# A fused attention and gated-MLP layer on one core: one hand-written order of all work, buffer places and load queues exchanged for another

## The chip, the cores and the metric

The kernel runs on one NeuronCore of a Trainium2 chip. A core has five engines that run side by side: PE (TensorE, matrix products), DVE (VectorE), ACT (ScalarE), POOL (GpSimd) and SP (SyncE, which here only issues DMA transfers). Each engine works through its own list of instructions strictly in order, and waits at an instruction until the semaphores that it names are up. The metric is the device time of one execution in microseconds (us). The kernel before takes 272.52 us, the median of three runs (272.19 to 273.63).

## The reference

Everything is bfloat16; S = 2048 rows, D = 640, H = 32 heads of 20, F = 1536.

```python
x = A_x
h  = x + A(layernorm(x))          # linear attention with a two-sided softmax feature map
h2 = h + B(layernorm(h))          # bilinear gated MLP, no nonlinearity
# A: q, k, v = split(x @ wqkv) by heads
#    pq = q @ w_phi[head];  pk = k @ w_phi[head]
#    phi_q = [softmax(pq), softmax(-pq)];  phi_k = [softmax(pk), softmax(-pk)]
#    kv = sum over rows phi_k^T v;  z = sum over rows phi_k
#    o = (phi_q @ kv) / (phi_q . z + 1e-6);  return o @ wo
# B: return ((x @ w_gate) * (x @ w_up)) @ w_down
```

## The kernel before

The 2048 rows are cut into 16 tiles t of 128 rows. Names of operations are a letter code and the tile's number; where a fold or a weight block is meant, the block's number.

- **Opening.** x0, x1, ... load rows; wk0 to wk4, wv0 to wv4, w5 (the feature matrices), wo, wg, wu, wd load weights. warm0 to warm19 are matmuls on zeros that nothing reads. WT0 to WT4 transpose the key weights on PE, WTe copies them out, Ph0 to Ph2 (POOL) spread the feature matrices, and F1_0 to F1_4 multiply the two ("fold"), so that one product gives pk directly; Fe1 copies the fold into the weight tile Wp. F0_0 to F0_4 do the same for the queries; their operand, the transposed query weights (tile scratch), comes by five DMA transposes wqt0 to wqt4, and each F0 waits for all five.
- **Norm and transposition.** L1s, L1a (DVE) take mean and variance of a tile, L1l and L1e (ACT) make the reciprocal deviation, L1n (POOL or DVE) the offset that an xn on ACT needs, xn scales the tile (DVE, or ACT with a longer instruction), xt transposes it into xnT: tiles 0 and 1 on PE with a copy xte, all others by a DMA transpose of SP.
- **Keys and values.** K, V on PE (ten matmuls of 320 columns each); Kx two exponentials on ACT, Ks the sums on DVE, Kr and Ke their reciprocal on ACT, Kn the product on POOL; Ve copies V out; KV adds the tile's contribution to the sum over rows. KVe0, KVe1 (DVE) close that sum, and all N need it.
- **Queries.** Q on PE, Qx (ACT), Qs (DVE), Qr (ACT), Qb (POOL), Qe (ACT), Qn (POOL), qT (DMA transpose), then N on PE; dd, rd, o on DVE, oT (DMA transpose), O on PE, h (DVE) adds to x; hc (ACT or DVE) and hT (DMA transpose) bring h into xnT for the MLP.
- **MLP.** For five blocks of rows (256, 512, 512, 512, 256) and twelve blocks of 128 inner columns: U_0 (gate) and U_1 (up) on PE, g copies the gate (ACT), u multiplies (DVE); then D on PE per tile, y (DVE), w stores.

No planner runs at build time. A table of text (PLAN) gives each operation a place in one global list, for some the engine (a second number), and the places of its PSUM banks or SBUF buffers (numbers behind the last colon). `arrange` sorts by that place; each engine's list is the sorted list cut down to that engine, and a wait is put in for each true dependence and each reuse of a buffer or bank. SP's list is at the same time the order in which SP issues transfers; loads whose second number is 1 are issued by ACT, or by SP where ACT is the first choice.

```python
        k, a, o.slots = PLAN.get(name, (key, 0, ()))
        o.eng, o.occ, o.lat = o.alts[a]
        ...
    for o in sorted(G.ops, key=lambda o: (o.key, o.i)):
```

Of the kernel before, what the change touches and what calls it, by code (L numbers as in the profile page):

```python
# [53 lines left out]
zero:0 x0:1:1 id0:2 w5:3:1 eps:4 warm0:5 gl0:6 x3:7:1 wk0:8 warm1:9 warm2:10 gla:11 wk1:12 warm3:13 id1:14 warm4:15 warm5:16 glb:17 x1:18 warm6:19 ekz:20  # L54
warm7:21 va1:22 wk2:23:1 warm8:24::0 warm9:25 wk3:26 warm10:27 warm11:28 wv0:29:1 warm12:30 L1s0:31 warm13:32 Ph0:33 wk4:34:1 warm14:35 warm15:36 warm16:37
x2:38 Ph1:39 L1a0:40 warm17:41 L1s3:42 WT1:43::7 L1l0:44 wv1:45 warm18:46 L1e0:47 Ph2:48 warm19:49 WTe1:50:1 wv4:51:1 xn0:52::3 Sz:53 mk0:54 wv3:55 L1a3:56
L1s1:57 phz:58 xt0:59::1 x4:60 F1_1:61::2 xte0:62 WT0:63::5 L1a1:64 wv2:65:1 WT2:66::0 L1l1:67 WTe0:68:1 x6:69 L1l3:70 WT3:71::7 L1e1:72 WTe2:73:1 Fe1_1:74
F1_0:75::4 xn1:76::3 F1_2:77::0 L1e3:78 Fe1_0:79:1 WTe3:80 L1n3:81 WT4:82::2 xt1:83::3 xn3:84::0 Fe1_2:85:1 F1_3:86::6 xte1:87:1 K0_0:88::4 xt3:89 Fe1_3:90
K0_1:91 WTe4:92:1 K0_2:93 L1s2:94 V0_0:95::0 F1_4:96::2 wqt0:97 V1_0:98::6 Fe1_4:99:1 V1_1:100 L1s4:101 K0_3:102 V1_2:103 K1_0:104::2 L1a2:105 L1s5:106
wqt3:107 L1l2:108 K1_1:109 K0_4:110 L1e2:111 K1_2:112 L1n2:113:1 L1a4:114 K1_3:115 L1a5:116 xn2:117::2 L1l4:118 K1_4:119 V0_1:120 L1e4:121 Kx0_0:122::0  # L60
xt2:123 V0_2:124 L1n5:125:1 L1n4:126 xn5:127::3 V0_3:128 Kx0_1:129 V0_4:130 L1s6:131 V1_3:132 Kx1_0:133::1 V1_4:134 x10:135 V3:136::4 L1s7:137 Kx1_1:138
xt5:139 Ve1:140::0 L1a6:141 xn4:142::0 K3:143::2 Ks0:144::0 Ve3:145::1 x8:146 Ve0:147::2 xt4:148 K2:149::4 L1a7:150 Ks1:151::1 L1l6:152 Kx3_0:153::2 wqt4:154
Kx3_1:155 V2:156::0 L1s11:157 L1e6:158 Kx2_0:159::3 L1n6:160 wqt1:161 L1n7:162 Kr0:163 Ks3:164::2 Kx2_1:165 K5:166::2 Ke0:167 Kr1:168 wqt2:169 Ve2:170::3
Kn0:171 xn6:172::3 V5:173::4 xn7:174:1:2 L1s9:175 xt6:176 Kx5_0:177::4 Ks2:178::3 V4:179::6 Ke1:180 Kx5_1:181 Kn1:182 xt7:183 Ve5:184::4 L1s8:185 F0_4:186::2
Kr2:187 Kr3:188 F0_3:189::0 Ke2:190 x14:191 Fe0_4:192:1 K4:193::4 Fe0_3:194 x12:195 L1a9:196 L1a8:197 Kn2:198 Ve4:199::5 Ks5:200::1 wo2:201 KV0:202::2,3
L1l8:203 L1e8:204 F0_2:205::0 Kx4_0:206::0 V6:207::6 L1n9:208:1 L1n8:209:1 xn9:210::0 Kx4_1:211 L1s10:212 rqz:213 xt9:214 Fe0_2:215 KV1:216 Ke3:217 L1a11:218
F0_0:219::4 Kr5:220 xn8:221::1 Kn3:222 K7:223::0 Fe0_0:224 Ks4:225::3 xt8:226 Ve6:227::0 F0_1:228::4 Kx7_0:229::1 L1a10:230 wg0:231 KV2:232 L1s14:233
K6:234::6 Kr4:235 wu1:236 mk1:237 Kx7_1:238 L1s15:239 Ke4:240 Fe0_1:241 Kn4:242 L1a14:243 KV3:244 Ks7:245::2 L1l10:246 K9:247::0 Kx6_0:248::3 Kx6_1:249
L1s13:250 L1e10:251 Ke5:252 Q0_0:253::4 Kx9_0:254::2 Q0_1:255 Kn5:256 L1n10:257:1 Q1_0:258::6 L1a13:259 L1s12:260 Kx9_1:261 Q1_1:262 Q0_2:263 Q1_2:264
xn10:265:1:0 L1a15:266 Q0_3:267 L1a12:268 Ks6:269::3 Q1_3:270 Q1_4:271 L1l12:272 xt10:273 Kr7:274 Q0_4:275 L1e12:276 Ke7:277 K8:278::0 L1n11:279 Qx1_0:280::3  # L70
Kn7:281 Ks9:282::1 Qx1_1:283 wo0:284 KV4:285 Kr6:286 wg2:287 Qx0_0:288::1 KV5:289 Qs1:290 Q3:291::6 Qx0_1:292 L1n13:293 L1n15:294 Ke6:295 Kx8_0:296::4
L1n12:297 Kn6:298 Qs0:299 V7:300::4 Kx8_1:301 Qr1:302::2 Qx3_0:303::0 xn13:304::1 Q5:305::0 Qx3_1:306 Ve7:307:1:5 xt13:308 Qb1:309 Qr0:310::0 Kr9:311
L1n14:312 xn15:313::2 Qb0:314 Ke9:315 mk2:316 KV6:317 Kn9:318 Qx5_0:319::2 Ks8:320::3 K10:321::6 wg1:322 xn11:323:1:3 Qs3:324 Qx5_1:325 Q2:326::4 xt11:327
Kr8:328 Qe1:329 smz:330 Kx10_0:331::3 Qn1:332 xn12:333::0 xt15:334 Q9:335::0 Ke8:336 Kx10_1:337 xn14:338::1 Qx2_0:339::4 Qs5:340 Kn8:341 xt12:342 KV7:343
Qx2_1:344 V8:345::6 Qr3:346::1 Qx9_0:347::5 Qs2:348 wg3:349 Qe0:350 K13:351::4 wu2:352 Qb3:353 Ve8:354::5 Qn0:355 Ks10:356::0 Qe3:357 Qx9_1:358 K11:359::6
Kx13_0:360::1 Qn3:361 Kx13_1:362 V9:363::0 Kx11_0:364::0 qT3:365::0 Qr2:366::3 Qr5:367::0 Kr10:368 Qb2:369 Qb5:370 KV8:371 Ke10:372 Kx11_1:373 Ve9:374:1:1
Kn10:375 K12:376::4 xt14:377 Ks13:378::3 V10:379::0 qT1:380::4 Kx12_0:381::4 Ks11:382::1 Kx12_1:383 K15:384::6 Qe5:385 Kr13:386 wd2:387 Ve10:388::6 Qn5:389
Ks12:390::0 qT0:391::1 Ke13:392 Kr11:393 Ke11:394 KV9:395 Qe2:396 Kn13:397 Q4:398::0 Kx15_0:399::2 Qs9:400 qT5:401::2 Kx15_1:402 K14:403::4 Qx4_0:404::0
Ks15:405::2 Kn11:406 Qx4_1:407 KV10:408 Qr9:409::1 V14:410::6 Kx14_0:411::3 Kr15:412 Ke15:413 wu0:414 Q10:415::0 Qb9:416 Ve14:417:1:7 Qn2:418 Qe9:419
Kx14_1:420 Qs4:421 V13:422::6 Kn15:423 Qx10_0:424::1 qT2:425::3 Kr12:426 Ks14:427::1 Ke12:428 Qr4:429::0 V12:430::4 Qx10_1:431 wu3:432 Ve13:433::3 Kn12:434  # L80
Kr14:435 V11:436::0 Ve12:437:1:6 Qs10:438 Q13:439::6 Ve11:440::0 Ke14:441 Kn14:442 V15:443::0 Qx13_0:444::3 Qx13_1:445 KV11:446 Ve15:447::5 Qs13:448 KV12:449
KV13:450 Qn9:451 Qr10:452::2 KV14:453 KV15:454 Q6:455::4 KVe0:456 Qb4:457 qT9:458::5 Qe4:459 Qn4:460 KVe1:461 Qx6_0:462::4 N0:463::2 N2:464::6 dd0:465::1
qT4:466::1 Qx6_1:467 Q7:468::0 rd0:469 dd2:470::0 o0:471::0 Qr13:472::3 rl2:473 Qb13:474 rd2:475 Qb10:476 o2:477::1 N1:478::4 Qx7_0:479::2 Q11:480::2
oT0:481::0 dd1:482::0 Qx7_1:483 rd1:484 o1:485::2 N9:486::6 oT2:487::1 Qx11_0:488::5 N3:489::0 dd9:490::0 Q8:491::4 rd9:492 Qx11_1:493 dd3:494::3 rd3:495
oT1:496::2 Qe13:497 o3:498::0 Qn13:499 O0:500::2 Qx8_0:501::0 oT3:502::3 o9:503::1 Qx8_1:504 O2:505::0 Qe10:506 h0:507 oT9:508::0 Qs7:509 hc0:510::3 N5:511::2
O1:512::4 qT13:513::2 h2:514 Qr7:515::3 Qb7:516 Qn10:517 O3:518::6 h1:519 hT0:520 hc1:521::2 N4:522::0 h3:523 Q14:524::4 L2q1:525 hT1:526 dd5:527::2
dd4:528::0 rl5:529 rd4:530 hc2:531::1 o4:532::1 O9:533::6 rd5:534 qT10:535::0 Qx14_0:536::3 o5:537::0 Qx14_1:538 Q12:539::0 h9:540 oT4:541::0 Qs14:542
U0_1_0:543::2 wd3:544 U0_0_0:545::6 g0_1:546::1 N13:547::4 oT5:548::3 U0_2_0:549::7 Qx12_0:550::1 dd13:551::1 Qs8:552 U0_0_1:553::2 g0_0:554::3 g0_2:555::0
hT2:556 U0_2_1:557::3 Qx12_1:558 U0_5_0:559::7 u0_0:560::0 Qr14:561::2 L2q2:562 rd13:563 Qb14:564 U0_1_1:565::6 wd1:566 hc3:567:1:0 O4:568::0 Qr8:569::0
u0_1:570 o13:571::2 u0_2:572 U0_3_0:573::6 Qs6:574 U0_4_0:575::2 g0_3:576::0 L2q0:577 O5:578::4 h4:579 Qe7:580 g0_5:581::1 Qn7:582 g0_4:583::2 U0_11_0:584::3  # L90
Qe14:585 hc4:586:1:3 h5:587 N10:588::0 U0_3_1:589::7 L2v1:590 qT7:591::2 Qn14:592 L2q5:593 U0_6_0:594::6 u0_3:595 U0_9_1:596::5 dd10:597::2 rd10:598 Qb8:599
hT3:600 U0_5_1:601::4 o10:602::1 L2v0:603 U0_4_1:604::7 U0_7_0:605::2 oT13:606::3 u0_4:607 Q15:608::0 L2v5:609:1 u0_5:610 g0_7:611::0 hc9:612:1:2 g0_6:613::3
hc5:614::1 hT4:615 U0_7_1:616::6 Qr6:617::3 Qx15_0:618::2 U0_6_1:619::7 hT5:620 Qx15_1:621 U0_8_0:622::2 u0_6:623 g0_11:624::2 U0_10_1:625::4 u0_7:626
L2q4:627 Qs12:628 U0_8_1:629::3 g0_8:630::3 U0_9_0:631::7 Qe8:632 Qn8:633 U0_10_0:634::0 u0_8:635 g0_9:636::1 L2q3:637 N7:638::1 U1_3_0:639::6 qT14:640::2
dd7:641::1 u0_9:642 Qb6:643 g0_10:644::3 rd7:645 Qe6:646 Qn6:647 o7:648::0 U1_1_1:649::7 qT8:650::0 L2r5:651 u0_10:652 U1_1_0:653::5 U1_0_1:654::3 oT7:655::0
U1_0_0:656::1 oT10:657::2 U1_2_1:658::0 g1_0:659::1 g1_3:660::0 hT9:661 u1_0:662::1 U1_2_0:663::1 Qs15:664 N8:665::2 g1_2:666::1 U1_7_0:667::6 g1_1:668::3
Qs11:669 U0_11_1:670::4 U1_9_0:671::5 dd8:672::0 u0_11:673 u1_1:674 U1_4_0:675::1 rd8:676 o8:677::0 U1_5_0:678::7 g1_4:679::3 u1_2:680 oT8:681::1 L2q9:682
# [809 lines left out]
```

## Time and profile before

| what | value |
|---|---|
| median of three runs | 272.52 us |
| time of the profiled execution | 272.19 us |
| its span (first to last instruction of the program) | 270.5 us |
| PE busy | 264.4 us, 98% |
| DVE, ACT, POOL busy | 157.0, 123.4, 70.7 us |
| DMA moved | 28.09 MB, mean 104 GB/s |

The span begins at the first instruction of any engine; the remaining 1.7 us of the profiled execution lie outside of it. A page row of waits reads "who waited, on what, total us, times, longest". A row of the timeline reads "start, length, engine, line, operation, number of instructions merged", and in brackets the idle time ahead of it with what the trace takes for its end. Matmul ends are modelled: a following matmul starts up to 0.16 us before the modelled end of the one before.

### The profile page before, as it was taken

How to read it: one execution, taken by the hardware profiler on the slowest of the kernel's cores; microseconds unless marked ns; L12 is line 12 of the kernel's file. 1: busy time of each engine (PE TensorE's matmuls, PEld its weight loads, DVE VectorE, ACT ScalarE, POOL GpSimd, SP SyncE). 2: the span in 40 equal slices, each digit the busy share in tenths (PEclk: the TensorE clock that was granted, in tenths of full speed). 3: DMA queues.
4: the chain of work that ended last, by engine and by line, in shares of the span. 5: the costliest groups of instructions: out<-in, count | busy, mean ns of one | idle time of the engine just before them, and what ended most of it. 6: DMA issues, size and time to landing. Idle time of an engine off the chain costs nothing.

```text
span 270.5 us, 5196 instructions
## 1 busy us (share of the span) xinstructions
PE 264.4 (98%) x2103; PEld 177.5 (66%) x2103; DVE 157.0 (58%) x296; ACT 123.4 (46%) x317; POOL 70.7 (26%) x86
## 2 busy tenths in 40 slices
...
GB/s 202 265 155 182 203 194 168 198 206 204 175 141 112 165 191 127 100 106 133 67 27 153 81 2 72 27 24 73 27 46 102 25 0 2 0 0 1 51 73 73
DMA packets 71752, 28.09 MB, mean 104 GB/s; under 512 B 59056, under 2 KB 71728, under 8 KB 71728
## 3 DMA queue, kind: packets, MB, share of 16 engines
...
q8 instruction: 16, 0.26, 0.4%
q10 hardware_dynamic: 288, 0.33, 0.4%
...
## 4 chain that ended last, share of the span: by engine, by line
PE 83%; DMA 6%; DVE 4%; ACT 3%; SPq 2%; POOL 1%; issue 1%; DVEq 0%
PE ps L646 39%; PE ps L665 19%; PE ps L460 14%; PE ps L603 8%; SPq L263 2%; DMA scratch<-ph 2%; DMA xnT<-xn 2%; DMA x_all<-in_A_x_dram 2%; PE ps L566 2%; ACT ek L472 1%; DVE SR L476 1%; POOL ek L496 1%; PE ps L504 1%; ACT ev L229 1%; DVE st L407 1%
## 5 line engine op out<-in xcount | busy, mean ns | idle before, releaser
L646 PE MATMUL ps<-xnT,Wgu 128*128 128x512 bf16 (+1 forms) x600 | 108.1, 336 | 0.2 <-issue 0.2
L646 PEld LDWEIGHTS ps<-xnT,Wgu 128*128 128x128 bf16 x600 | 58.0, 98 | 42.7 <-DVE ev L654 0.8
L651 ACT ACTIVATE gt<-ps 128x512 bf16<-128x512 f32 (+1 forms) x60 | 29.3, 511 | 97.1 <-PE ps L646 86.1
L460 PE MATMUL ps<-Wp,xnT 128*128 128x320 bf16 (+1 forms) x480 | 68.6, 299 | 0.2 <-DMA xnT<-xn 0.2
L654 DVE TENSOR_TENSOR ev<-ps,gt 128x512 bf16<-128x512 f32 (+1 forms) x60 | 34.0, 579 | 57.7 <-PE ps L646 43.5
L460 PEld LDWEIGHTS ps<-Wp,xnT 128*128 128x128 bf16 x480 | 45.5, 97 | 17.6 <-DMA xnT<-xn 0.3
L665 PE MATMUL ps<-Wd,ev 128*128 128x320 bf16 (+2 forms) x396 | 53.8, 295 | 0.0
L665 PEld LDWEIGHTS ps<-Wd,ev 128*128 128x128 bf16 x396 | 38.2, 98 | 15.4
L496 POOL TENSOR_TENSOR ek<-ek,SR 128x1280 bf16<-128x1280 bf16 x16 | 37.5, 2360 | 3.8 <-ACT SR L481 3.7
L548 POOL TENSOR_TENSOR ph<-ph,RQ 128x660 bf16<-128x660 bf16 x16 | 20.9, 1311 | 28.6 <-ACT RQ L544 28.5
L677 DVE SCALAR_TENSOR_TENSOR Wp<-ps,rs,x_all 128x640 bf16<-128x640 f32 (+3 forms) x18 | 14.3, 806 | 22.7 <-PE ps L665 20.2
L534 DVE TENSOR_REDUCE S<-ph 128x66 f32<-128x1320 bf16 x16 | 24.1, 1520 | 2.1 <-ACT ph L531 2.0
L603 PE MATMUL ps<-Wo,Wp 128*128 128x320 bf16 x160 | 23.5, 299 | 0.0
L529 ACT ACTIVATE ph<-ps 128x600 bf16<-128x600 f32 x32 | 21.4, 683 | 4.0 <-PE ps L460 2.6
L476 DVE TENSOR_REDUCE SR<-ek 128x64 f32<-128x1280 bf16 x16 | 23.2, 1464 | 0.0
L472 ACT ACTIVATE ek<-ps 128x640 bf16<-128x640 f32 x32 | 21.4, 708 | 1.7 <-PE ps L460 1.3
L609 DVE SCALAR_TENSOR_TENSOR x_all<-ps,x_all 128x640 bf16<-128x640 f32 x16 | 13.1, 821 | 12.4 <-PE ps L603 12.4
L603 PEld LDWEIGHTS ps<-Wo,Wp 128*128 128x128 bf16 x160 | 15.6, 98 | 6.6 <-issue 0.2
L624 POOL TENSOR_SCALAR ln<-mv 128x1 f32<-128x1 f32 x6 | 1.2, 192 | 62.3 <-ACT ek L620 62.0
L593 DVE TENSOR_TENSOR o<-ps,sm 128x660 bf16<-128x660 f32 x16 | 13.4, 843 | 4.3 <-ACT sm L586 3.3
L620 ACT ACTIVATE ek<-x_all,mv 128x640 bf16<-128x640 bf16 x16 | 13.2, 823 | 1.2 <-DVE x_all L609 1.2
L618 ACT ACTIVATE xn<-x_all,mv 128x640 bf16<-128x640 bf16 x10 | 8.1, 822 | 6.1 <-DVE x_all L609 6.1
...
## 6 DMA issues: line engine op xcount, KB each, us to landing
...
```

The costliest lines, as they stand in the source:

```text
L460: ins = e.matmul(pb(b, hb)[:, 0:n1 - n0], lhsT=T["xnT"][:, NC - 1 - c, P * t:P * (t + 1)], rhs=T["Wp"][:, POS[kind], c, n0:n1], start=(c = ...
L472: G.op("act", "%sx%d_%d" % (nm, t, s), lambda e, s=s, b=b, ek=ek: e.activation(out=T["ek"][:, ek.slots[0], 0:2 * D].rearrange("p (b h s f) ...
L476: G.op("dve", "%ss%d" % (nm, t), lambda e, ek=ek, sr=sr: e.tensor_reduce(out=T["SR"][:, sr.slots[0], 0, :], in_=T["ek"][:, ek.slots[0], 0: ...
L496: G.op("pool", "Kn%d" % t, lambda e, eng, ek=ek, sr=sr: e.tensor_tensor(out=T["ek"][:, ek.slots[0], 0:2 * D].rearrange("p (h f) -> p h f", ...
L529: e.activation(out=v[:, 0:10].rearrange("p (b g) j f -> p b g j f", b=2), in_=pp(b, 0, 300).rearrange("p b (g j f) -> p b g j f", j=3, f=D ...
L534: G.op("dve", "Qs%d" % t, lambda e, t=t, ph=ph: e.tensor_reduce(out=T["S"][:, t, 0:66].rearrange("p (g k) -> p g k", k=6), in_=pv(ph).rear ...
L548: return e.tensor_tensor(out=v, in0=v, in1=T["RQ"][:, rq.slots[0], 1, 0:33].rearrange("p (g j) -> p g j", j=3).unsqueeze(3).to_broadcast([ ...
L603: ins = e.matmul(pb(b, hb)[:, 0:320], lhsT=T["oT"][:, oT.slots[0], c, :], rhs=T["Wo"][:, c, 320 * hb:320 * (hb + 1)], start=(c == 0), stop ...
L646: ins = e.matmul(pb(b)[:, 0:n], lhsT=T["Wgu"][:, gu, c, P * ft:P * (ft + 1)], rhs=T["xnT"][:, NC - 1 - c, o0:o0 + n], start=(c == 0), stop ...
L651: G.op("act", "g%d_%d" % (bi, ft), lambda e, pg=pg, gt=gt, n=n: e.activation(out=T["gt"][:, gt.slots[0], 0:n], in_=pb(pg)[:, 0:n], func=AF ...
L654: o_ = G.op("dve", "u%d_%d" % (bi, ft), lambda e, pu=pu, gt=gt, hh=hh, ft=ft, n=n: e.tensor_tensor(out=T["hh"][:, hh.slots[0], ft, 0:n], i ...
L665: ins = e.matmul(pb(b, hb)[:, 0:w], lhsT=T["hh"][:, hh.slots[0], ft, P * tt:P * (tt + 1)], rhs=T["Wd"][:, ft, c0 + w * hb:c0 + w * (hb + 1 ...
```

## The change

Only the table is exchanged. The operations, their shapes, their number on each engine's arithmetic and the pools are the same; what differs is the place of every operation, the engine of those with a choice, the buffers, and which queue issues the first loads. The new table has one line of text more, so every line below it has a number higher by one. Of the old and the new table, the beginning, and the places of the fourteenth key tile:

```diff
@@ PLAN, first words
-zero:0 x0:1:1 id0:2 w5:3:1 eps:4 warm0:5 gl0:6 x3:7:1 wk0:8 warm1:9 warm2:10 gla:11 wk1:12
+zero:0 mk0:1 wk1:2:1 x0:3 gl0:4 warm0:5 w5:6 wk0:7:1 id0:8 warm1:9 warm2:10 id1:11 x3:12 x1:13
...
@@ the fourteenth key tile, PE's words alone
-K14:403:4 ... KV10:408 V14:410:6 Q10:415:0 V13:422:6 V12:430:4 V11:435:0 Q13:439:6 V15:443:0 KV11:446
+K14:405::0 ... KV10:411 Q10:414:4 V15:417:2 V12:426:0 V11:432:4 Q13:436:2 V14:441:4 KV11:444
```

SP's list from the first load on. x_all is the tile of the rows, ev holds the key weights here, Wp<-in_A_wqkv the value weights, xnT<-xn an xt, scratch<-in_A_wqkv a wqt. Before:

```order
L263 DMA w5<-in_A_w_phi_dram 128x5x20
L263 DMA x_all<-in_A_x_dram 128x640
L263 DMA ev<-in_A_wqkv_dram 128x640
L263 DMA x_all<-in_A_x_dram 128x640
L263 DMA ev<-in_A_wqkv_dram 128x640 x2
```

Now:

```order
L264 DMA x_all<-in_A_x_dram 128x640
L264 DMA ev<-in_A_wqkv_dram 128x640
L264 DMA x_all<-in_A_x_dram 128x640
L264 DMA ev<-in_A_wqkv_dram 128x640 x3
L264 DMA Wp<-in_A_wqkv_dram 128x640
```

w5 and x3 have left SP's list and x0 and wk0 have entered it: ACT issues wk1, w5, x3 now, and issued x0 and wk0 before.

SP's list further on, from xt3 to xt7. Before:

```order
L449 DMA_TRANSPOSE xnT<-xn 128x5x128
L287 DMA_TRANSPOSE scratch<-in_A_wqkv_dram 128x1x640 x2
L449 DMA_TRANSPOSE xnT<-xn 128x5x128
L263 DMA x_all<-in_A_x_dram 128x2x640
L449 DMA_TRANSPOSE xnT<-xn 128x5x128
L263 DMA x_all<-in_A_x_dram 128x2x640
L449 DMA_TRANSPOSE xnT<-xn 128x5x128
L287 DMA_TRANSPOSE scratch<-in_A_wqkv_dram 128x1x640 x3
L449 DMA_TRANSPOSE xnT<-xn 128x5x128 x2
```

Now:

```order
L450 DMA_TRANSPOSE xnT<-xn 128x5x128
L288 DMA_TRANSPOSE scratch<-in_A_wqkv_dram 128x1x640 x2
L450 DMA_TRANSPOSE xnT<-xn 128x5x128
L264 DMA x_all<-in_A_x_dram 128x2x640 x2
L450 DMA_TRANSPOSE xnT<-xn 128x5x128
L288 DMA_TRANSPOSE scratch<-in_A_wqkv_dram 128x1x640 x3
L450 DMA_TRANSPOSE xnT<-xn 128x5x128 x3
```

The order before is xt3, two wqt, xt2, x10, xt5, x8, xt4, three wqt, xt6, xt7; now both x loads stand ahead of xt5, and the last three wqt ahead of xt4.

ACT's list at its start (L229 and L230 are copies out of PSUM, L429 and L430 an xn). Before:

```order
L414 ACTIVATE ln<-mv,eps 128x1
L417 ACTIVATE rs<-ln 128x1
L229 ACTIVATE scratch<-ps 128x5x128
L229 ACTIVATE xnT<-ps 128x5x128
L414 ACTIVATE ln<-mv,eps 128x1 x2
L417 ACTIVATE rs<-ln 128x1
L229 ACTIVATE Wp<-ps 128x640
L417 ACTIVATE rs<-ln 128x1
L229 ACTIVATE Wp<-ps 128x640 x4
```

Now:

```order
L415 ACTIVATE ln<-mv,eps 128x1
L418 ACTIVATE rs<-ln 128x1
L230 ACTIVATE scratch<-ps 128x5x128
L415 ACTIVATE ln<-mv,eps 128x1
L230 ACTIVATE scratch<-ps 128x5x128
L230 ACTIVATE Wp<-ps 128x640
L415 ACTIVATE ln<-mv,eps 128x1
L418 ACTIVATE rs<-ln 128x1 x2
L230 ACTIVATE Wp<-ps 128x640
L430 ACTIVATE xn<-x_all,nb,rs 128x5x128
L230 ACTIVATE Wp<-ps 128x640
```

xn3 has come from DVE to ACT, behind WTe1, WTe0, Fe1_1 and Fe1_0; WTe0 and WTe4 have come to ACT as well, while xte0 and Fe1_2 have gone to DVE. On PE, the first query folds F0_0 and F0_4 stand behind six products of ten matmuls (V3, K3, V2, K2, V5, K5), where seven (V4 too) stood ahead of the first of them before.

More of the change, by code (lines that the diff above doesn't have):

```diff
@@ L53 @@
 for _t in """
[L54 to L97, printed above, removed]
@@ L122 @@
-D13_0:1004::6 y14_0:1005::0 w14_0:1006 w8_0:1007 D12_0:1008::2 y13_0:1009::2 w13_0:1010 w7_0:1011 D11_0:1012::6 y12_0:1013::0 y15_0:1014::2 w12_0:1015
-D10_0:1016::2 y11_0:1017::1 w11_0:1018 w15_0:1019 D15_1:1020::1 y10_0:1021::0 w10_0:1022 D15_2:1023::6 y15_1:1024::1 w15_1:1025 y15_2:1026::2 w15_2:1027
+zero:0 mk0:1 wk1:2:1 x0:3 gl0:4 warm0:5 w5:6 wk0:7:1 id0:8 warm1:9 warm2:10 id1:11 x3:12 x1:13 warm3:14 warm4:15 gla:16 warm5:17 wk2:18:1 glb:19 warm6:20
+eps:21 phz:22 warm7:23 wk3:24 warm8:25::5 warm9:26 wk4:27:1 warm10:28 warm11:29 wv0:30:1 warm12:31 warm13:32 L1s0:33 x2:34 warm14:35 warm15:36 Ph0:37
@@ new lines @@
+WT1:38::1 wv1:39 warm16:40 L1a0:41 warm17:42 L1s3:43 Ph1:44 x4:45 L1l0:46 L1e0:47 WTe1:48:1 wv2:49:1 Ph2:50 xn0:51::0 wv4:52:1 L1a3:53 rqz:54 va1:55 WT0:56::2
+L1l3:57 x6:58 xt0:59::1 L1s1:60 WTe0:61 F1_1:62::6 WT2:63::0 wv3:64 Fe1_1:65 xte0:66:1 F1_0:67::2 L1a1:68 WT3:69::4 WTe2:70:1 L1l1:71 warm18:72 L1e3:73
+WT4:74::6 WTe3:75 L1e1:76 Fe1_0:77:1 L1n3:78 warm19:79 F1_2:80::0 ekz:81 xn1:82::1 F1_3:83::4 smz:84 xn3:85:1:0 Sz:86 Fe1_2:87 K0_0:88::2 K0_1:89 xt1:90::7
+Fe1_3:91 L1s2:92 xt3:93 K0_2:94 V0_0:95::0 WTe4:96 V0_1:97 xte1:98:1 K0_3:99 L1a2:100 L1s5:101 V0_2:102 wqt2:103 L1l2:104 F1_4:105::4 L1e2:106 K1_0:107::6
```

89 lines of the change are left out of this document (65 added, 24 removed).

## The prediction

> **What bounds the kernel now.** I read the page first, for the share of each engine, and then the waits of PE alone.
>
> ```profile
> span 270.5 us, 5196 instructions
> ...
> PE 264.4 (98%) x2103; PEld 177.5 (66%) x2103; DVE 157.0 (58%) x296; ACT 123.4 (46%) x317; POOL 70.7 (26%) x86
> ```
>
> ```profile
> PE ps L345 <- DVE ev L343: 1.1, 1, 1.1
> PE ps L370 <- DMA ev<-in_A_wqkv_dram: 0.8, 1, 0.8
> PE ps L389 <- ACT SR L481: 0.5, 1, 0.5
> PE ps L440 <- DVE xn L431: 0.4, 1, 0.4
> PE ps L566 <- DMA scratch<-ph: 0.3, 1, 0.3
> PE ps L646 <- issue: 0.2, 1, 0.2
> PE ps L460 <- DMA xnT<-xn: 0.2, 1, 0.2
> ```
>
> PE bounds the kernel: it is busy for 264.4 of 270.5 us. Its waits come to 3.5 us in seven places, 2.3 us of which (L345, L370, L440) lie before its first product of real size. The change takes no matmul away, so the most it can win is these 3.5 us (1.3%) and stalls inside of what counts as busy; what it can lose is open. The question is whether the new order keeps PE fed. The timeline of PE shows two of these places:
>
> ```profile
> 6.53 0.45 PE L440 MATMUL ps<-ident,xn 128*128 128x128 bf16 x5 [0.44 <-DVE xn L431]
> ...
> 25.83 0.80 PE L389 MATMUL ps<-Phi,scratch 128*128 128x140 bf16 x12 [0.55 <-ACT SR L481]
> 26.47 1.52 PE L460 MATMUL ps<-Wp,xnT 128*128 128x320 bf16 x10
> 27.83 0.50 PE L504 MATMUL ps<-ev,ek 128*128 128x63 bf16 x11
> ```
>
> The row at 6.53 is xt0, at 25.83 F0_4 and F0_3, at 26.47 K4, at 27.83 KV0; of the waits above, L460 is K9 and L566 is N9. From start to start, a product of ten matmuls takes 1.36 us (26.47 to 27.83) and a fold 0.32 us (25.83 to 26.47, two of them). The row at 25.83 names ACT, but F0_4 also waits for all five wqt, and the rows below say that the last of them landed 0.2 us before it: the wait is for a DMA.
>
> **The opening and SP's chain.** Both hang on SP's list. Its rows for x3, wk1, x1, xt3, xt4 and the last three wqt:
>
> ```profile
> 1.32 0.51 SPq L263 DMA_DIRECT2D x_all<-in_A_x_dram  x1
> 1.88 0.42 SPq L263 DMA_DIRECT2D ev<-in_A_wqkv_dram  x1
> 2.35 0.43 SPq L263 DMA_DIRECT2D x_all<-in_A_x_dram  x1
> ...
> 9.97 1.31 SPq L449 DMA_TRANSPOSE xnT<-xn  x1
> ...
> 18.62 1.20 SPq L449 DMA_TRANSPOSE xnT<-xn  x1
> 19.86 3.90 SPq L287 DMA_TRANSPOSE scratch<-in_A_wqkv_dram  x3
> ```
>
> From issue to landing the views by tile give, for the three wqt, for xt4, for the next two xt (xt6, xt7), for x3 and for x1, in this order:
>
> ```profile
> DMA to landing us min/median/max: 3.1/3.8/4.5
> DMA to landing us min/median/max: 3.9/3.9/3.9
> DMA to landing us min/median/max: 2.6/2.7/2.7
> DMA to landing us min/median/max: 3.7/3.7/3.7
> DMA to landing us min/median/max: 3.4/3.4/3.4
> ```
>
> The last wqt is issued at 22.49 (a third of the 3.90 before that row's end) and lands 3.1 later, at 25.6; F0_4 starts at 25.83. The whole chain begins with xt3 at 9.97, as soon as xn3 is there.
>
> *When does xn3 come now?* It hangs on xn0, and xn0 on x3, since DVE keeps the order L1s0, L1s3, xn0. x3 landed at 1.32 + 3.7 = 5.0; it is now ACT's third load, issued after two others where it was SP's second. Of full-sized loads, x0 and wk0 shared its way before, and x0, wk1, wk0 and x1 do now. The nearest row is the load that had as many ahead of it, x1, which landed at 2.35 + 3.4 = 5.75; on the other side both queues now carry full loads from 0.8 us on, where SP began with the small w5. So x3 lands between 4.9 and 5.75, and I take 5.0, as before, so that xt0 stays near 6.5. From xn0 on ACT's list runs L1l3, WTe0, Fe1_1, L1l1, L1e3, L1e1, Fe1_0, xn3. Rows of such instructions:
>
> ```profile
> L229 ACT ACTIVATE Wp<-ps 128x640 bf16<-128x640 f32 x9 | 6.1, 700 | 1.8 <-PE ps L389 1.8
> ...
> L429 ACT ACTIVATE xn<-x_all,nb,rs 128x640 bf16<-128x640 bf16 x3 | 2.8, 927 | 0.0
> ```
>
> Three copies of 0.60 (0.70 less the 0.1 by which neighbours overlap), four short ones of together 0.7 and an xn of 0.93 are 3.4 us behind xn0's end, which the row at 6.53 puts at 6.48: xn3 at 9.9. Before, xt3 was issued at 9.97. So the chain starts level (0.0; -0.1 to +0.8 by x3). What PE gains in the opening (WT0 runs ahead of xt0, while warm18 and warm19, 0.2 us, go behind it) is then given back at F0_0, because SP's chain, not PE, sets that time.
>
> *F0_0.* Between xt3 and the last wqt the chain loses only the xt4 (1.20 and a step of 0.04); both x loads stay in. The last wqt is issued at 22.49 - 1.24 = 21.25 and lands 3.1 to 4.5 later; with 0.2 to PE's start, F0_0 runs at 24.55 to 25.95. Only six products stand ahead of it, so 25.83 - 1.36 = 24.47 would be level. I take 24.8, nearer to the short end because the third of three landed fastest: **+0.3** (+0.1 to +1.5). K4 follows after two folds, at 25.4; xt4 is issued at 22.5 and lands by the row 3.9 later at 26.4, or 2.7 later, as xt6 and xt7 do, at 25.2: **+0.1** (0 to +1.0). The 0.2 at K9 goes, since xt9 no longer has the load wo2 just ahead of it and K9 stands two of Q1's five parts (0.5 us) later: **-0.2**. Next late would then be V5, whose xt5 stands behind two x loads now.
>
> **35 to 72 us.** PE has no idle time here, but ACT, DVE and POOL have little either:
>
> ```profile
> 40.00:50.00 10.00, 10.00 (x110) 7.49 (x108) 9.92 (x11) 9.95 (x33) 10.00 (x13) 1.00 0.75 186
> 50.00:70.00 20.00, 20.00 (x175) 14.65 (x173) 16.11 (x14) 16.19 (x49) 18.33 (x14) 1.00 0.94 208
> ```
>
> After the stretch and its length, the columns are PE, PEld, DVE, ACT, POOL. ACT gets one xn more (xn3, xn4, xn9, xn13 for xn7, xn10, xn11), 0.9 us, mostly before 40, and two V copies more (Ve7, Ve9, Ve12, Ve14 come, Ve4 and Ve10 go), 1.4 us. Behind 50 us ACT has 3.8 us free and covers the copies. POOL's work up to the last Kn is the same: sixteen Kn, five Qn. Cost 0, and up to +2.3 if ACT's free time lies in the wrong place.
>
> **The hand-over from keys to queries.** Kn14 is POOL's last key product in both orders, Qn9 and qT9 follow, and PE's list from KV11 to N9 is the same:
>
> ```profile
> 72.34 1.85 PE L504 MATMUL ps<-ev,ek 128*128 128x63 bf16 x55
> ```
>
> ```profile
> 70.74 2.35 POOL L496 TENSOR_TENSOR ek<-ek,SR 128x1280 bf16<-128x1280 bf16 x1 [0.32 <-ACT SR L481]
> 73.06 1.31 POOL L548 TENSOR_TENSOR ph<-ph,RQ 128x660 bf16<-128x660 bf16 x1
> ```
>
> ```profile
> 74.39 5.22 DMA scratch<-ph
> ```
>
> The first row is KV11 to KV15, the next two are Kn14 and Qn9, the last, from the chain that ended last, is qT9. At 0.34 each KV14 starts at 73.36; Kn14 ends at 73.09: 0.27 in hand. K14 now stands six products before KV11 instead of seven (the words of PLAN), so KV14 comes 1.36 sooner after K14. But Kn14 comes sooner too: ahead of Ke14, ACT has Ve15, Ve12, Ve11, and V11 ends four products after K14, not five as before. Level; **+0.1** for the lost slack, -0.3 (the wait at L566 gone) to +0.6 by qT9's landing, whose 5.22 are one sample of many such transposes.
>
> **MLP and end: 0.** The nearest distances on PE's list grow or stay, counted in matmul time: O1 to the first U 5.4 us (5.8 before), tile 8's O to block 2 6.5 (the shortest there was 6.0). wu1 is loaded late now, behind qT7, some 5 us of SP's list ahead of U0_3_1, about what a load takes to land; it may be late by a few tenths. At the end D11 starts one D of 1.63 us after the last U, where 3.26 stood before; the two u that it waits for take less:
>
> ```profile
> 250.09 1.29 DVE L654 TENSOR_TENSOR ev<-ps,gt 128x512 bf16<-128x512 f32 x2 [2.02 <-PE ps L646]
> ```
>
> D10, D15_1, D15_2 and their stores stand as before. The range for both parts is -0.3 to +0.8.
>
> **Instruction transfers.** The change names them, so I weigh them apart.
>
> ```profile
> q8 instruction: 16, 0.26, 0.4%
> ```
>
> 0.4% of 16 engines' 270.5 us over 16 packets is 1.1 us each, on one DMA engine; a load with a share behind it lands up to 1.1 later. The places shift with the order, and which load is hit can't be told from the trace: 0, with up to +1.1 if it is the wqt or qT9. [...]
>
> **The sum**: 0.0 + 0.3 + 0.1 - 0.2 + 0.1 = +0.3 on the profiled execution's 272.19 gives 272.5. That execution was the fastest of three; the median was 0.33 above it, so as a median 272.8.
>
> **The rivals.** 0.5% (1.36 us) is about what a measurement of this kernel can tell from no change.
>
> *Slower: the opening is late.* x3 lands at 5.75 and xn3 0.75 later; SP's chain moves with it, the last wqt takes the median 3.8 to land, and F0_0 comes at 21.25 + 0.75 + 3.8 + 0.2 = 26.0, 1.2 behind my 24.8, and K4 waits 0.3 more for an xt4 that is late too: 272.8 + 1.5 = 274.3. It decides once F0_0 starts after 25.9 (24.8 and 1.1 to the bound). For it speaks that x3 has one load more ahead; against, that the DMA engines start on full loads sooner. Chance 0.20.
>
> *Slower: ACT becomes the bound* between 35 and 70 us, 2.3 us more work on a full engine: 272.8 + 2.3 = 275.1. Against it: 3.8 us free behind 50. Chance 0.10.
>
> *Faster.* Full loads from the first issue on bring x3 by 4.6, SP's chain starts 0.4 sooner, and F0_0 runs at 24.0 (0.8 off my 24.8); K4 does not wait (0.1), qT9 lands in 4.5 (0.4 with the lost slack), and the wait of L646 (0.2) and some stalls inside of U (0.3) go: 272.8 - 1.8 = 271.0. For it speaks the idle time of the DMA queues ahead of x3; against, that five things must go well. Chance 0.17.
>
> That the change does not do what it says is no case here: the lists shown are other lists. The forecast, within 0.5% (271.2 to 273.9), has the rest, 0.53. The range of 271.0 to 275.2 leaves half of the faster case below, and half of the ACT case above; alone, the forecast's is 271.8 to 273.9.
>
> **What would show it.** Right: F0_0 within 24.4 to 25.4, waiting for scratch from the query weights; no idle PE between 35 and 72; N9 within 0.6 of its transpose. Wrong: F0_0 after 25.9, PE idle behind L472 copies or exponentials in 35 to 72, L646 waiting on Wgu, or L665 on DVE at the end.

## The result, and the profile after

The new order is slower: 274.61 us in the median of twenty executions (273.34 to 275.45), against 272.56 in the median of twenty executions of the kernel before. The ratio is 1.0069, with a 95% interval of 1.0053 to 1.0084, so about 1.9 us. The executions of one kernel scatter by 2 us, and the profiled one was the fastest of the twenty (273.34), so its trace shows less of the loss than most: 1.1 us in the span. A second profile of the same kernel, below, is of a usual execution. Six of the twenty executions have a granted PE clock of 0.994 over their span; the other fourteen, at 0.999 or 1.00, still have a median of 274.46, so the clock is not what makes the new order slower.

The page of the new kernel, span and first row of the engines:

```profile
span 271.6 us, 5200 instructions
...
PE 264.5 (97%) x2103; PEld 177.4 (65%) x2103; DVE 157.7 (58%) x297; ACT 121.4 (45%) x315; POOL 70.7 (26%) x87
```

PE still does the same 264.5 us of work; what has grown is the time in which it waits. PE's waits:

```profile
PE ps L441 <- DVE xn L432: 1.8, 1, 1.8
PE ps L346 <- DVE ev L344: 1.1, 1, 1.1
PE ps L390 <- DMA scratch<-in_A_wqkv_dram: 0.8, 1, 0.8
PE ps L604 <- DMA Wp<-o: 0.5, 1, 0.5
PE ps L567 <- DMA scratch<-ph: 0.3, 1, 0.3
```

They sum to 4.5 us, 3.5 before. The first row (xt0 waiting for xn0) was 0.4 and is 1.8; the 0.8 for wk1 (L370 before) is gone, since wk1 comes first now. L390 is F0_0, L604 is O0, which did not wait before. The places on PE's timeline:

```profile
7.28 0.45 PE L441 MATMUL ps<-ident,xn 128*128 128x128 bf16 x5 [1.83 <-DVE xn L432]
...
25.57 0.81 PE L390 MATMUL ps<-Phi,scratch 128*128 128x140 bf16 x12 [0.83 <-DMA scratch<-in_A_wqkv_dram]
26.28 1.53 PE L461 MATMUL ps<-Wp,xnT 128*128 128x320 bf16 x10
...
73.18 1.91 PE L505 MATMUL ps<-ev,ek 128*128 128x63 bf16 x55
...
80.49 0.85 PE L567 MATMUL ps<-KVm,scratch 128*128 128x63 bf16 x22 [0.28 <-DMA scratch<-ph]
...
83.20 2.89 PE L604 MATMUL ps<-Wo,Wp 128*128 128x320 bf16 x20 [0.49 <-DMA Wp<-o]
```

These rows let the loss be placed. Ahead of K4 (26.28) the new list has one product of 1.36 us less than the old one (V4 comes behind it now), and as many folds; so 26.47 - 1.36 = 25.11 would be level, and K4 is 1.17 late. From KV11 on, the same work stands ahead in both lists: KV11 is 73.18 - 72.34 = 0.84 late, N9 80.49 - 79.66 = 0.83, and the span is 1.1 longer. The rows of before for N9 and O0:

```profile
79.66 0.85 PE L566 MATMUL ps<-KVm,scratch 128*128 128x63 bf16 x22 [0.33 <-DMA scratch<-ph]
...
81.72 2.88 PE L603 MATMUL ps<-Wo,Wp 128*128 128x320 bf16 x20
```

So the loss is there by 26 us; a part comes back by KV11, O0's wait adds again (O0 is 83.20 - 81.72 = 1.48 late), and the MLP gives some back.

Four rows of the chain that ended last say where it begins (start, length, what):

```profile
1.74 4.07 DMA x_all<-in_A_x_dram
...
6.72 0.52 DVE xn L432
...
21.88 3.64 DMA scratch<-in_A_wqkv_dram
...
78.78 4.37 DMA Wp<-o
```

The first row is x3: issued by ACT at 1.74, it lands at 5.81 instead of 5.06. xn0, the second row, ends at 7.24 (6.48 before). xn3 on ACT ends at 10.67, and SP issues xt3 at 10.69. From there SP's issues stand back to back:

```profile
10.69 1.30 SPq L450 DMA_TRANSPOSE xnT<-xn  x1
12.04 3.25 SPq L288 DMA_TRANSPOSE scratch<-in_A_wqkv_dram  x2
15.34 1.27 SPq L450 DMA_TRANSPOSE xnT<-xn  x1
16.66 1.09 SPq L264 DMA_DIRECT2D x_all<-in_A_x_dram  x2
17.80 1.22 SPq L450 DMA_TRANSPOSE xnT<-xn  x1
19.06 4.10 SPq L288 DMA_TRANSPOSE scratch<-in_A_wqkv_dram  x3
23.20 3.92 SPq L450 DMA_TRANSPOSE xnT<-xn  x3
```

These are xt3, two wqt, xt2, x8 and x10, xt5, three wqt, and xt4 with xt6 and xt7. The third row of the chain is the last wqt: it lands at 25.52, and F0_0 starts. xt4 lands at 26.24, just ahead of K4. The last row of the chain is oT0, for which O0 waits.

And the stretches in which ACT might have become the bound; after the stretch and its length come PE, PEld, DVE, ACT, POOL:

```profile
40.00:50.00 10.00, 10.00 (x92) 7.31 (x90) 10.00 (x13) 9.56 (x32) 8.72 (x9) 1.00 0.47 119
50.00:70.00 20.00, 20.00 (x189) 14.69 (x186) 15.23 (x13) 17.65 (x52) 19.52 (x16) 1.00 1.01 214
```

PE has no idle time there, as before. ACT has 1.1 us more to do in these 30 us (27.21 against 26.14), about half of the 2.3 that the prediction counted for it.

### The profile page after: what moved, and what is told of

Its sections match the earlier page's. It is cut to its first block, busy times and chain, and to the rows that moved or that the text cites. A ratio compares the mean times of both kernels' runs of the same rounds, so it can differ in the third digit from the quotient of the medians.

```text
span 271.6 us, 5200 instructions
## 1 busy us (share of the span) xinstructions
PE 264.5 (97%) x2103; PEld 177.4 (65%) x2103; DVE 157.7 (58%) x297; ACT 121.4 (45%) x315; POOL 70.7 (26%) x87
## 4 chain that ended last, share of the span: by engine, by line
PE 88%; DMA 4%; DVE 4%; SPq 1%; ACT 1%; issue 0%; ACTq 0%; DVEq 0%
PE ps L647 38%; PE ps L666 19%; PE ps L461 18%; PE ps L604 8%; PE ps L505 2%; DMA Wp<-o 2%; DMA x_all<-in_A_x_dram 1%; PE ps L567 1%; DMA scratch<-in_A_wqkv_dram 1%; SPq L288 1%; PE ps L390 1%; DVE st L407 1%; DVE st L408 1%; DVE xn L432 1%; DVE SR L477 1%; ACT ph L530 0%
## 5 line engine op out<-in xcount | busy, mean ns | idle before, releaser
L604 PE MATMUL ps<-Wo,Wp 128*128 128x320 bf16 x160 | 23.9, 299 | 0.5 <-DMA Wp<-o 0.5
L604 PEld LDWEIGHTS ps<-Wo,Wp 128*128 128x128 bf16 x160 | 15.3, 98 | 7.2 <-DMA Wp<-o 0.8
L230 ACT ACTIVATE ev<-ps 128x640 bf16<-128x640 f32 x14 | 9.8, 714 | 1.4 <-PE ps L461 1.4
```

The source lines that it names most:

```text
L604: ins = e.matmul(pb(b, hb)[:, 0:320], lhsT=T["oT"][:, oT.slots[0], c, :], rhs=T["Wo"][:, c, 320 * hb:320 * (hb + 1)], start=(c == 0), stop ...
```

## The experiments

**Theory O**, from these rows: the opening is late, because x3 lands late and SP's list carries that to F0_0 and K4. **Theory H**: the loss comes from the hand-over from keys to queries and from the MLP, where O0 waits. Four kernels join one table's beginning to the other's end. The buffers that reach across the joint were given one name in both.

*Old opening, new rest*, and *new opening, old rest*, joined at V3 (15.6 us before):

```diff
@@ PLAN, words ahead of V3
-zero:0 mk0:1 wk1:2:1 x0:3 gl0:4 warm0:5 w5:6 wk0:7:1 id0:8 ... (new)
+zero:0 x0:1:1 id0:2 w5:3:1 eps:4 warm0:5 gl0:6 x3:7:1 wk0:8 ... (old)
@@ from V3 on: new
```

> The table's first part (all that stands ahead of V3) as before, the rest as after. Theory O (the loss is made in the opening: x3 late, so xn3, SP's chain and F0_0 late): xt0 back at 6.5 us, F0_0 near 24.8, total 273.0 to 273.6, at least 1.0 us below after's 274.6. Theory H (the loss is made at the hand-over or behind it): total stays 274.2 to 274.9, whatever the opening does.

Measured: 273.16 us, ratio 1.0015 (0.9993 to 1.0037), as Theory O had it. x3 lands at 4.84 and xt0 starts at 6.33; F0_0, expected near 24.8, starts at 25.34 behind a wait of 0.34.

```diff
@@ PLAN, words ahead of V3
-... (old)
+... (new)
@@ from V3 on: old
```

> The opposite: ahead of V3 as after, the rest as before. Theory O: xt0 near 7.3, total 273.4 to 274.2 (before and 0.8 to 1.6). Theory H: 272.3 to 273.0, as before.

Measured: 274.03 us, ratio 1.0037 (1.0017 to 1.0056). x3 lands at 5.75, the last query weights at 27.18, and F0_4 starts at 27.42. Both kernels also have a wait of 0.8 to 0.9 us for ACT behind the joint, at 16 to 17 us, which neither table has by itself; PE still waits for the query weights behind it, so it is largely absorbed there.

*The same, joined at KV11* (72.3 us before), so that norm, keys and values are of one table, and the hand-over and the MLP of the other:

```diff
@@ PLAN, words ahead of KV11
-... (new)
+... (old)
@@ from KV11 on: new
```

> All that stands ahead of KV11 (opening, keys, most queries) as before, the hand-over and the MLP as after. Theory O: 272.3 to 273.0, as before. Theory H: 273.4 to 274.6, with PE waiting for oT0 at O0 as in after.

Measured: 272.86 us, ratio 0.9993 (0.9968 to 1.0017), and in its trace PE doesn't wait at O0.

```diff
@@ PLAN, words ahead of KV11
-... (old)
+... (new)
@@ from KV11 on: old
```

> All that stands ahead of KV11 as after, the hand-over and the MLP as before. Theory O: 273.8 to 274.9, as after. Theory H: 272.6 to 273.6, with O0 not waiting.

Measured: 274.61 us, ratio 1.0059 (1.0040 to 1.0079). x3 lands at 6.30, and K4 starts at 27.48.

What follows: the new hand-over and MLP by themselves cost nothing that can be told from zero, and with the old ones the loss stays. H falls. The loss lies ahead of KV11. Of it, 0.37% comes with the new words ahead of V3 alone, and 0.54% goes when only these are put back (1.0069 against 1.0015); the rest comes with the words from V3 to KV11, or lies within the intervals.

**Is it the first loads?** The next two exchange only the order and the queues of the six first loads.

```diff
@@ new table: words of the first loads, at the same places
-wk1::1 x0 w5 wk0::1 x3 x1      (ACT: wk1, w5, x3; SP: x0, wk0, x1)
+x0::1 w5::1 x3::1 wk0 wk1 x1   (ACT: x0, wk0; SP: w5, x3, wk1, x1)
```

> The new table, with the six first loads (x0, w5, x3, wk0, wk1, x1) in the old order and on the old queues; all else as in the new table. Theory O (x3's place in its queue makes the opening late, and that is carried to F0_0): x3 lands at 4.9 to 5.2, xt0 starts at 6.4 to 6.6, xt3 is issued at 9.8 to 10.1, the last query weights land at 24.6 to 25.1, and F0_0 starts at 24.7 to 25.2; the ratio to the kernel before is 1.003 to 1.0045. Rival B (the lists of ACT and PE behind the loads make it late, xn3 on ACT above all): xt3 still comes at 10.4 or later, F0_0 at 25.4 or later, ratio 1.006 to 1.008.

Measured: 274.57 us, ratio 1.0073 (1.0050 to 1.0097): no gain, and outside Theory O's 1.003 to 1.0045. And yet the loads did what O said: x3 landed at 4.96, xt3 was issued at 10.06, the last query weights landed at 24.44, and F0_0 started at the time that is level (24.47). PE's timeline shows what came next:

```profile
24.48 0.81 PE L393 MATMUL ps<-Phi,scratch 128*128 128x140 bf16 x12 [0.16 <-DMA scratch<-in_A_wqkv_dram]
25.95 1.53 PE L464 MATMUL ps<-Wp,xnT 128*128 128x320 bf16 x10 [0.66 <-DMA xnT<-xn]
```

The row at 25.95 is K4: it waits 0.66 us for xt4, which the new table issues behind the last three wqt. F0_0 was early by 1.09 against the profile of the new kernel, K4 by only 0.33. This profiled execution (272.95) was also the fastest of six, of which four lie at 274.57 or above.

```diff
@@ old table: words of the first loads, at the same places
-x0::1 w5::1 x3::1 wk0 wk1 x1
+wk1::1 x0 w5 wk0::1 x3 x1
```

> The old table, with the six first loads in the new order and on the new queues; all else as in the old table. Theory O: x3 lands at 5.7 to 5.9, xt3 is issued at 10.6 to 10.8, the last query weights land at 26.0 to 27.2 and F0_4 starts 0.2 behind them; ratio to the kernel before 1.003 to 1.005. Rival B: the old lists absorb it, xt3 at 10.2 or earlier, F0_4 at 26.0 or earlier, ratio below 1.0015.

Measured: 273.86 us, ratio 1.0063 (1.0039 to 1.0086), x3 at 6.27, xt3 issued at 12.11, F0_4 at 28.25, all later, like the ratio, than either theory had them. The new first loads alone slow the old table. Its profiled execution (275.35) was one of its slowest, and shows something more, to which the last section comes back: PE's clock fell to 0.50 after a wait of 2.45 us. The six of its twelve executions whose granted clock is 1.00 have a median of 273.22, 0.35% above the kernel before, which is what Theory O expected of the late x3.

**Why does x3 land late?** ACT's queue with x3 ahead of w5:

```diff
@@ new table
-w5:6 ... x3:12
+x3:6 ... w5:12
```

> The new table, with x3 and w5 exchanged in ACT's queue: wk1, x3, w5. Theory P (x3 is held up by the load in front of it in its own queue, w5 with its many small packets): x3 lands at 4.7 to 5.2 instead of 5.8, w5 at 5.3 to 5.8 instead of 4.9. Theory Q (all loads in flight share the DMA engines, so a place in a queue moves little): x3 lands at 5.5 to 5.8. As the fold needs w5, PE's first fold can then start no earlier than 7.1 to 7.6, so that xt3 comes only 0.1 to 0.5 earlier than its 10.7 under P, and the ratio to the kernel before is 1.004 to 1.007 under either.

Measured: x3 lands at 4.67, w5 at 7.19; 275.25 us, ratio 1.0105 (1.0078 to 1.0133). ACT's issues, and the view of w5's tile:

```profile
0.84 0.40 ACTq L267 DMA_DIRECT2D ev<-in_A_wqkv_dram  x1
1.27 0.45 ACTq L267 DMA_DIRECT2D x_all<-in_A_x_dram  x1
1.75 0.46 ACTq L267 DMA_DIRECT2D w<-in_A_w_phi_dram  x1
```

```profile
DMA to landing us min/median/max: 5.4/5.4/5.4
```

P held for x3: with w5 out of its way it lands 1.1 to 1.6 us earlier, 0.5 of it by its earlier issue. But w5 paid more than P allowed: 5.4 us behind two full loads, where it took 3.7 behind one (new kernel) and 2.6 at the head of SP's queue (kernel before). The first fold then waited 2.15 us for it, xt3 came at 12.08, and the table as a whole got slower than either theory had it.

**Is it the length of SP's chain?** The next kernel was to have x8 and x10 issued by ACT, and its expectation was written for that. What ran is another edit: both stay on SP, behind xt5.

```diff
@@ new table, SP's words
-xt2 x8 x10 xt5 wqt4 wqt3 wqt0 xt4
+xt2 xt5 x8 x10 wqt4 wqt3 wqt0 xt4
```

> The new table, with the loads x8 and x10 issued by ACT at the same places instead of SP; all else as in the new table. They take 1.14 us of SP's time ahead of xt5 and the last three query weights. Theory C (SP's chain of issues sets F0_0): x3 lands at 5.8 as in the changed kernel, xt5 is issued at 16.8 to 17.0, so that V5 doesn't wait, the last query weights land at 24.3 to 24.6 and F0_0 starts at 24.5 to 24.8; ratio to the kernel before 1.002 to 1.004. Rival D (what the DMA engines move, not the issue on SP, sets the landing of the query weights): they land at 25.2 or later, F0_0 at 25.4 or later, ratio 1.006 to 1.008.

Measured: 274.58 us, ratio 1.0078 (1.0051 to 1.0106). It can't speak on the two theories as they stand there, but it shows another thing: xt5 lands at 19.85 instead of 21.81, so V5 doesn't wait (it waits 0.44 in the usual execution of the new table, below), and nothing is won, since F0_0 and K4 wait instead:

```profile
25.64 0.81 PE L393 MATMUL ps<-Phi,scratch 128*128 128x140 bf16 x12 [1.01 <-DMA scratch<-in_A_wqkv_dram]
26.98 1.53 PE L464 MATMUL ps<-Wp,xnT 128*128 128x320 bf16 x10 [0.53 <-DMA xnT<-xn]
```

So V5, F0_0 and K4 stand behind one another on the same chain, and time won at the first is given back at the next. The last four therefore take the two x loads out of the chain altogether: SP issues nothing from about 7.5 us to xt3, and there they go.

```diff
@@ new table, SP's words; the first loads as in the new table
-x6 wv3 xt3 wqt2 wqt1 xt2 x8 x10 xt5 wqt4 wqt3 wqt0 xt4
+x6 wv3 x8 x10 xt3 wqt2 wqt1 xt2 xt5 wqt4 wqt3 wqt0 xt4
```

> The new table, with the loads x8 and x10 ahead of xt3 in SP's list; the first loads stay as in the new table. Theory C: x3 lands at 5.7 to 6.3, xt3 is issued at 10.6 to 11.2, the last query weights land at 24.1 to 24.9, F0_0 starts at 24.3 to 25.1, xt4 lands at 25.3 to 26.1 and K4 starts with it; ratio to the kernel before 1.002 to 1.0045, about 1 us less than the new table. Rival D: as above, ratio 1.006 or above.

Measured: 272.99 us, ratio 1.0018 (0.9997 to 1.0039). x3 lands at 5.72, xt3 is issued at 10.61, as late as in the new kernel; yet the last query weights land at 24.14, 1.4 earlier than in its first profile, and the timeline of PE has

```profile
24.20 0.80 PE L393 MATMUL ps<-Phi,scratch 128*128 128x140 bf16 x12
25.24 1.53 PE L464 MATMUL ps<-Wp,xnT 128*128 128x320 bf16 x10 [0.24 <-DMA xnT<-xn]
```

F0_0 doesn't wait, and K4 is 0.13 from level: Theory C held, with F0_0 and xt4 0.1 earlier than it said, and D falls. The seven of its twelve executions with a granted clock of 1.00 have a median of 272.44, against 272.66 of the kernel before beside them: there the loss is gone, with x3 as late as in the new kernel. The unchanged new table ran beside it:

> The new table unchanged, as the yardstick for the two edits of it, and as a second look at its opening, since its first profile was of its fastest execution. Expected of a usual execution: x3 at 5.8 to 6.3, F0_0 at 25.6 to 26.3, xt4 landing at 26.2 to 27.5 and K4 waiting for it by up to 0.7; ratio to the kernel before 1.005 to 1.0085.

Measured: 274.21 us, ratio 1.0071 (1.0050 to 1.0093). The profiled execution (274.13) is a usual one. Its waits and its timeline of PE:

```profile
PE ps L441 <- DVE xn L432: 1.6, 1, 1.6
PE ps L346 <- DVE ev L344: 1.1, 1, 1.1
PE ps L461 <- DMA xnT<-xn: 1.1, 2, 0.7
PE ps L604 <- DMA Wp<-o: 0.3, 1, 0.3
PE ps L567 <- DMA scratch<-ph: 0.2, 1, 0.2
PE ps L647 <- DMA Wgu<-in_B_w_up_dram: 0.2, 1, 0.2
```

```profile
22.66 2.89 PE L461 MATMUL ps<-Wp,xnT 128*128 128x320 bf16 x20 [0.44 <-DMA xnT<-xn]
25.60 0.81 PE L390 MATMUL ps<-Phi,scratch 128*128 128x140 bf16 x12
27.07 1.53 PE L461 MATMUL ps<-Wp,xnT 128*128 128x320 bf16 x10 [0.66 <-DMA xnT<-xn]
```

x3 lands at 6.30 here. V5 waits 0.44 for xt5 and K4 0.66 for xt4; F0_0 starts where it did in the first profile, but waits for nothing more, since V5's wait comes ahead of it. K4 is 1.96 behind level and the span, 272.4, is 1.9 longer than before: the whole measured loss. Against this, moving the two loads wins 0.53%, 1.4 us.

The same two loads moved in the other two kernels:

```diff
@@ old table, SP's words
-wv2 x6 xt3 wqt0 wqt3 xt2 x10 xt5 x8 xt4 wqt4 wqt1 wqt2
+wv2 x6 x10 x8 xt3 wqt0 wqt3 xt2 xt5 xt4 wqt4 wqt1 wqt2
```

> The old table, with the loads x8 and x10 ahead of xt3 in SP's list. Theory C: the last query weights land 1.1 us earlier, at 24.4 to 24.7, F0_4 no longer waits (0.5 us at 25.83 before) and K9's wait stays; ratio to the kernel before 0.997 to 0.9995. Rival D: xt3 lands a us later, V3 waits, ratio 1.001 or above.

Measured: 272.06 us, ratio 0.9979 (0.9964 to 0.9994), faster than both kernels. The waits of PE that are left:

```profile
PE ps L349 <- DVE ev L347: 1.1, 1, 1.1
PE ps L374 <- DMA ev<-in_A_wqkv_dram: 1.0, 1, 1.0
PE ps L393 <- ACT scratch L233: 0.3, 1, 0.3
PE ps L570 <- DMA scratch<-ph: 0.3, 1, 0.3
PE ps L650 <- issue: 0.2, 1, 0.2
```

The 0.5 at F0_4 is gone, as expected. Not as expected, the last query weights land at 25.17 instead of 24.4 to 24.7: wk1 landed 0.67 later in this execution than in the profile of before, and xt3 was issued 0.5 later. Of Rival D one half shows: xt3 lands at 16.32, 1.9 later than before. But V3 waits only 0.11 for it, and the ratio is Theory C's. The 0.2 at K9, which was to stay, is gone too.

```diff
@@ new table: both edits
-(first loads of the new table; x8 x10 behind xt2)
+(first loads of the old table; x8 x10 ahead of xt3)
```

> The new table with two edits: the six first loads in the old order and on the old queues, and the loads x8 and x10 ahead of xt3 in SP's list, where SP issues nothing, instead of between xt2 and xt5. Theory C (the time from xn3 on is set by SP's chain: its start by x3, its length by what stands between the transposes; it sets V5, the first F0 and K4 in turn): xt3 is issued at 9.9 to 10.2, xt5 at 16.0 to 16.3, the last query weights land at 23.3 to 23.9 and xt4 at 24.6 to 25.0, so that neither V5 nor F0_0 nor K4 waits or only K4 does, up to 0.2; the ratio to the kernel before is 0.997 to 1.001. Rival D (the DMA engines are the limit, and two loads more in the opening push the transposes back): xt3 lands 1.0 us later or more, V3 waits for it, and the ratio is 1.003 or above.

Measured: 273.26 us, ratio 1.0027 (1.0010 to 1.0044), no better than with x8 and x10 early alone, and a miss. x3 landed at 4.58, but xt3 was issued only at 11.23. The reason is in the first row of PE's opening:

```profile
5.64 0.71 PE L374 MATMUL ps<-ident,ev 128*128 128x128 bf16 x5 [0.93 <-DMA ev<-in_A_wqkv_dram]
```

The same five matmuls take 0.45 in the kernel that has only the first loads exchanged (5.38 us there): 0.71 is also what they take in the last section at a granted clock of 0.50. PE stayed as slow until about 10.1 us (0.69 to 0.74 for five transposes, 0.44 behind that), and xn3 stands behind the copies of PE's transposes and folds on ACT's list; it ends at 11.21.

The table puts the runs together whose order at K4 is the new one. Level for K4 is 25.11; the last column is the span less K4's lateness.

| kernel | x3 lands | xt3 issued | F0_0 | xt4 lands | K4 | span | ratio | span - (K4 - 25.11) |
|---|---|---|---|---|---|---|---|---|
| new | 5.81 | 10.69 | 25.57 | 26.24 | 26.28 | 271.6 | 1.0069 | 270.4 |
| new, again | 6.30 | 11.18 | 25.60 | 27.03 | 27.07 | 272.4 | 1.0071 | 270.4 |
| old ahead of V3 | 4.84 | 10.10 | 25.34 | 25.80 | 25.98 | 271.2 | 1.0015 | 270.3 |
| new ahead of KV11 | 6.30 | 11.19 | 26.11 | 27.44 | 27.48 | 272.8 | 1.0059 | 270.4 |
| first loads old | 4.96 | 10.06 | 24.48 | 25.91 | 25.95 | 271.2 | 1.0073 | 270.4 |
| x8, x10 behind xt5 | 5.99 | 10.88 | 25.64 | 26.94 | 26.98 | 273.0 | 1.0078 | 271.1 |
| x3 ahead of w5 | 4.67 | 12.08 | 26.69 | 27.92 | 27.97 | 273.3 | 1.0105 | 270.4 |
| x8, x10 early | 5.72 | 10.61 | 24.20 | 25.20 | 25.24 | 271.0 | 1.0018 | 270.9 |
| both edits | 4.58 | 11.23 | 25.38 | 25.82 | 26.02 | 272.0 | 1.0027 | 271.1 |

The span before is 270.5. Whatever was edited, what is left after taking off K4's lateness is 270.3 to 271.1: nearly the whole loss of the new table is made by 27 us, ahead of K4. What makes K4 late is not the same in every row: a late x3 and SP's list in most of them, w5's fold where x3 stands ahead of w5, PE's slow opening in the last. Nor do the runs divide the loss between x3 and the list: x3 put right alone wins nothing in the median (1.0073), and the two x loads moved alone win 0.53% with x3 as late as it was.

## Why the prediction was right in its range and wrong in its forecast

It said the same within 0.5%, 272.8 us, and the new table is slower by 0.69%. The time of 274.61 lies in its range only because the range took in the slower rivals; the forecast itself missed. The first of these rivals, "the opening is late" at 274.3 with a chance of 0.20, named the mechanism: x3, SP's chain, F0_0, and K4 behind a late xt4. Its sign did not show, though: F0_0 started at 25.57 and 25.60, neither within 24.4 to 25.4 (right) nor after 25.9 (wrong). The sign was set at F0_0, and the loss shows at K4. Point by point:

- **"x3 lands between 4.9 and 5.75, and I take 5.0": this is the first step that failed.** x3 landed at 5.81 and 6.30 in the two profiles, above both ends. The bounds counted full-sized loads ahead and took the end of w5 as nothing but a small load that no longer leads SP's queue. But w5 now stands in front of x3 in ACT's queue, and x3 ahead of w5 lands at 4.67. The trace of before had a hint: w5 alone, 25 KB at the head of SP's queue, took 2.6 us to land, over two thirds of the 3.7 of x3. The term of the sum that this set, the start of the chain, stood at 0.0.
- **xn0 to xn3, 3.4 us.** Right: xn0 ends at 7.24 and xn3 at 10.67, 3.43 apart. The lateness of x3 went through in full, as the rival had it, and the "0.0" became +0.7 (xt3 at 10.69 against 9.97; +1.2 in the second profile).
- **F0_0 at 24.8, +0.3.** It started at 25.57, +1.10 against level. The way from xt3's issue to the last wqt's was foreseen as 1.24 shorter and is 1.33 shorter (9.97 to 22.49 before, 10.69 to 21.88 now); the landing was put at 3.35 and took 3.64. Both fine; what was mis-sized is the start.
- **K4 +0.1: the second step that failed.** Mis-sized too, and by a wrong question. xt4 behind the three wqt was weighed only as an addition to a nearly punctual F0_0. K4 is the last link of the same chain, and even with x3 on time (the kernel with the old first loads) it waits 0.66: xt4 lands 3.4 after its issue there, between the 2.7 and the 3.9 that were weighed. In the usual execution K4, not F0_0, is what waits, and its lateness of 1.96 is the loss. V5, named as late next, waits 0.44 there.
- **K9 -0.2, no idle PE from 35 to 72 us, the hand-over +0.1.** Right: no wait at K9; PE busy 10.00 of 10.00 and 20.00 of 20.00; N9 waits 0.28 (0.33 before), and KV11 to KV15 take 1.91 where they took 1.85. The rival in which ACT becomes the bound did not happen.
- **MLP and end 0.** Right as a sum. wu1 is late by 0.2 in the usual execution (0.5 with x8 and x10 early), as "a few tenths" said; this is the one sign of being wrong that did show. What I did not see is oT0: O0 waits 0.3 to 0.5 for it. Before, oT0 was issued at 77.57 and landed 3.7 later. It is issued 1.21 later now (0.8 of that is PE's lateness) and lands 4.37 later, as the row of the chain says. By the span the MLP gives most of that back, and the kernel with the old table ahead of KV11 and the new one behind it is level, 0.9993; in its trace O0 doesn't wait at all.
- **Instruction transfers 0.** No run shows this 0. In the trace of before and in the new kernel's first profile none starts between 0.2 and 11.3 us, so x3 is not late by them there. Behind that, some fall among the transposes (one at 24.41 in the first profile, while the last query weights and xt4 are on their way; one at 22.91 before); what they cost there no run separates.

The sum was +0.3. With the measured sizes of the first profile it reads +1.17 at K4 (x3 and SP's chain together), about -0.3 by KV11, +0.65 at O0 and -0.35 in the MLP: +1.1, the difference of the spans.

What stays open: putting back the first loads alone did not lower the median (1.0073), though its one profile shows a K4 1.1 us earlier than in the usual execution of the new table. Its executions fall in two groups, 273.0 to 273.5 and 274.6 to 274.9. A granted clock that falls, as in the last section, is not it: all six have 1.00. A PE that stays slow through the opening, as in the kernel with both edits, does not show in that figure (it reads 1.00 in that kernel, too) and would make a step of this kind (xt3 comes 1.2 later there), but there is no trace of an execution of the upper group, so this is argued and not shown. Nor is it shown why x3, on the same place of the same queue, lands at 5.7 to 6.3 from one profile to the next.
